# Linear attention and a gated unit on one core: the products of v and the folds of k of chunk 0 written out in one order for three engines

## The chip, the cores and the metric
The kernel runs on one core of one Trainium2 chip. The time is the device time of one execution, in microseconds. The core has a matrix engine (PE, TensorE) that writes to eight banks of PSUM, a vector engine (DVE), a scalar engine (ACT), a third elementwise engine (POOL, GpSimd) and SP (SyncE), which here issues all DMAs.

## What is computed
All inputs are float32; x is 2048 x 1024. `xn` is x normalized row by row. Two branches come from it:

```python
xn = layernorm(x)
q, k, v = split(xn @ wqkv)                     # 32 heads of 32
phi(a) = [softmax(a @ w_phi), softmax(-(a @ w_phi))]   # per head
o = phi(q) @ (phi(k).T @ v) / (phi(q) @ sum(phi(k)) + 1e-6)
s = o @ wo
g = silu((sigmoid(xn @ w_gate) * (xn @ w_up)) @ w_down)
out = x + s * g
```

## The kernel before
**Products.** A float32 value is split into a high part, a cast to PE's reduced float type (ACT, L126), and the rest, the value minus the high part (DVE, L127). `mm3` (L129 to L133) then makes three matmuls of 128 x 128 by 128 x 512 of one product: high by high, high by low, low by high. Every large matrix product is done block by block with seven products in place of eight (B11, T2, T3, B21, T1, T4, B22), whose operands are sums and differences of the blocks of both sides. B21 adds to the bank of B11, T4 to that of T3, B22 to that of T1, so each of these must wait until the first result has been read out.

**Stages.** The 2048 rows are two chunks of 1024. Chunk 0 goes through the projections v, k, q (in this order, `PROJ`), seven products each in the order B11, B21, T2, T3, T4, T1, B22 (`order`, L289), and then the gated unit; chunk 1 follows, with attention work laid in between; then `w_down`, the attention output and `wo`. One of the seven products of a projection has four banks (`u`, 128 rows each) of four `mm3` each: 48 matmuls. `proj_out` (L384 on) reads the banks: ACT copies B11 and B21 (L396, L399), DVE adds the others up (L393) and SP stores results to `qkv_d`.

**The opening.** The kernel starts on raw x. `norm` (L156 to L179) takes statistics of a tile of 128 rows on DVE (L163, L164), a square root on ACT (L169), a reciprocal on DVE (L170), six small operations on POOL (L172 to L177) and one normalization of 1024 columns on ACT (L179). `transpose` (L189 to L201) has PE turn a tile in eight 128 x 128 transposes (L195) and ACT copy them out (L199). `x_sums` (L203 to L209) makes the operands T1 to T4 of x: T2 and T3 on DVE, T1 and T4 on POOL. `v_sums` (L250 to L257) makes those of the weights of v, half on DVE and half on POOL, 1024 columns at a time. The weights of k and q are first multiplied by `w_phi`, once for all: `fold` (L274 to L285) loads four blocks of 128 x 512, has PE multiply each by block-diagonal `bd` in four matmuls (L283), copies the results (L284), and `w_sums` (L225 to L234) stores three blocks as they are, makes four sums in place on POOL (L229 to L232) and stores these, all to `wf_d`. The first sum overwrites the fourth block, which has been stored before. Four such `fold(K, k)` and four `fold(Q, k)` fill what is needed; the folds of q use slots (50, 51) and (52, 53) in turn.

**What sets the order.** The entries of `side`, in the order x tiles, `v_sums`, x tiles, four folds of k, the remaining operands of x (`x_rest`), four folds of q, are started one by one by `step()` after each bank of v's products, so all of them are done within v. A scheduler then puts the instructions of each engine in one order; `issue_after` bars an instruction from standing ahead of another. `prep` (L338 on) loads and splits weights for the products to come, as far as a ring of eight slots (28 to 35) has room. During k, after B11, T2, T4 and B22 (n = 7, 9, 11, 13), one task of `bg2` is started each time: `o_sums` (L261 to L271), which loads four raw blocks of `wo` into slots (52, 53) or (45, 46) by turns, splits three of them, makes four sums of them on POOL, splits these too, and stores each of the seven splits to `wo_d` from one of four slots (`o_split`: 54, 36, 37, 38). Before it starts, PE is warmed with 28 transposes of the identity (L729).

Of the kernel before, what the change touches and what calls it, by code (L numbers as in the profile page):

```python
# [48 lines left out]
def hedgehog_glu_kernel(  # L49
# [19 lines left out]
    make_identity(nc, ident)  # L69

# [35 lines left out]
    WARM = 28  # L106
# [17 lines left out]
    def split(o, src):  # L124

        nc.scalar.copy(o[0], src)  # L126
        return nc.vector.tensor_sub(o[1], src, o[0].bitcast(F32))  # L127
# [22 lines left out]
    last_norm, last_chain = [], []  # L150

    def x_load(t, slot):
        nc.sync.dma_start(whole(slot), x[t * P:(t + 1) * P, :])
        return whole(slot)

    def norm(tiles, xs):  # L156
        n = len(tiles)
        st = small.tile([P, 2, 2, 6], F32, name=f"bn{tiles[0]}", tag="bn")
        mv = small.tile([P, 2, 2], F32, name=f"mv{tiles[0]}", tag="mv")
        ws = small.tile([P, 4, 2], F32, name=f"lnw{tiles[0]}", tag="lnw")  # L160
        for i, xt in enumerate(xs):
            for a in range(2):
                nc.vector.bn_stats(st[:, i, a], xt[:, a * HB:(a + 1) * HB])  # L163
            nc.vector.bn_aggr(mv[:, :, i], st[:, i])  # L164
        v, r, a, b = [ws[:, q, :n] for q in range(4)]
# [4 lines left out]
        nc.vector.reciprocal(r, a)  # L170

        eng.tensor_mul(a, r, r)  # L172
# [4 lines left out]
        last_chain[:] = [eng.tensor_scalar(b, b, -1.0, None, op0=ALU.mult).ins]  # L177
        for i, xt in enumerate(xs):
            last_norm[:] = [nc.scalar.activation(xt, xt, AF.Identity, bias=b[:, i:i + 1], scale=r[:, i:i + 1]).ins]  # L179

    def operand(c, i, u, b):

        if c == 0:
            o, cs = run(XO[i], 4), slice(u * P, (u + 1) * P)
            split((o[:, :, 0, cs], o[:, :, 1, cs]), b.rearrange("p (k t) -> p k t", t=P))
        else:
            nc.sync.dma_start(xo_d[i, :, u], b)

    def transpose(t, xt, dst):  # L189

        c, th, u = t // CTT, t % CTT // 4, t % 4
        for q in range(2):
            tp = tps.next()
            for k in range(4):
                nc.tensor.transpose(tp[:, k * P:(k + 1) * P], xt[:, (4 * q + k) * P:(4 * q + k + 1) * P], ident)  # L195
            i = {(0, 0): B11, (1, 0): B21, (1, 1): B22}.get((q, th))
            if c == 0 and th == 0:
                operand(c, i, u, tp)
            nc.scalar.copy(dst[q], tp)  # L199
            if c and i is not None:  # L200
                operand(c, i, u, dst[q])  # L201

    def x_sums(c, u, first, second):  # L203
        (b11, b21), (b12, b22) = first, second
        t2 = b22 if c else b12
        for i, o, a, b in ((T1, b11, b12, b11), (T3, b12, b22, b12), (T2, t2, b22, b11), (T4, b21, b21, t2)):
            (nc.vector if c == 0 and i in (T2, T3) else nc.gpsimd).tensor_sub(o, a, b)
            if c or i in (T2, T3):
                operand(c, i, u, o)  # L209
# [12 lines left out]
    fraw = Ring(halves(43, 11))  # L222
    fblock = {K: Ring(((4, 5), (6, 7))), Q: Ring(((50, 51), (52, 53)))}
# [13 lines left out]
    VA = (39, 41, 45, 36)  # L237
    v_first = {B11: 39, B21: 41, T2: 39, T3: 45, T4: 39, T1: 36, B22: 41}
# [4 lines left out]
    def v_block(f, kh):  # L243
        return wv[kh * HB:(kh + 1) * HB, f * HB:(f + 1) * HB].rearrange("(k p) n -> p k n", p=P)
# [5 lines left out]
    def v_sums():  # L250
        vec, pool = nc.vector.tensor_tensor, nc.gpsimd.tensor_tensor
        for f, o, a, b, op in ((vec, 3, 2, 3, "add"), (vec, 2, 0, 2, "subtract"),
                               (pool, 0, 3, 0, "subtract"), (pool, 1, 1, 0, "subtract")):
            for h in range(2):
                f(whole(VA[o] + h), whole(VA[a] + h), whole(VA[b] + h), op=getattr(ALU, op))
        for i in (T2, T3, T1, B22):
            nc.sync.dma_start(wf_d[V, i], row4(v_first[i]))  # L257
# [15 lines left out]

    def fold(which, k):  # L274

        bs = halves(*fblock[which].next())
        for b, (f, h) in zip(bs, ((0, 0), (0, 1), (1, 0), (1, 1))):
            r = fraw.next()
            nc.sync.dma_start(r, wqkT[which, f, k + 4 * h].rearrange("p g n -> p (g n)"))
            ps = tps.next()  # L280
            for g in range(4):
                gs = slice(g * P, (g + 1) * P)
                nc.tensor.matmul(ps[:, gs], r[:, gs], bd[:, 4 * f + g], start=True, stop=True)  # L283
            nc.scalar.copy(b, ps)  # L284
        w_sums(lambda i, b: nc.sync.dma_start(wf_d[which, i, :, k], b), *bs)  # L285
# [52 lines left out]
    def prep():  # L338
# [9 lines left out]
        if kind == "proj":  # L348
            h = len(ready[n]) // 2
            if h == 0:  # L350
                here = c == 0 and what == V
                proj_src[n] = r = v_first[i] if here else proj_raw.next()
                if what == V and i in (B11, B21, T4) and not (here and i != T4):
                    nc.sync.dma_start(row4(r), v_block(*{B11: (0, 0), B21: (0, 1), T4: (1, 1)}[i]))
                elif not here:
# [153 lines left out]
    def x_task(t):  # L509
        xt = x_load(t, 52)  # L510
        norm([t], [xt])
        th, u = t % CTT // 4, t % 4
        transpose(t, xt, halves(53 + th))
        if th:
            x_sums(t // CTT, u, halves(53), halves(54))
# [178 lines left out]
    XS = (24, 25, 26, 27, 52, 53, 24, 25)  # L694
    first = [halves(i) for i in (50, 51, 54, 38)]
    b12s, b22s = Ring(halves(10)), halves(8, 9)
    xts = [x_load(0, XS[0])]
    phraw = whole(47)[:, :KT * DH].rearrange("p (g f) -> p g f", f=DH)
    nc.sync.dma_start(phraw, w_phi.rearrange("(g p) f -> p g f", p=P))
    v_load(0)  # L700
    xts += [x_load(t, XS[t]) for t in range(1, 4)]
    v_load(1)
    xts += [x_load(t, XS[t]) for t in range(4, 6)]

    def x_tiles(*tiles):
        norm(tiles, [xts[t] for t in tiles])
        for t in tiles:
            if t < 4:
                transpose(t, xts[t], first[t])
            else:  # L710
                b = b12s.next(), b22s[t - 4]
                transpose(t, xts[t], b)
                x_sums(0, t - 4, first[t - 4], b)
            if t < 2:
                xts.append(x_load(t + 6, XS[t + 6]))
            if t == 1:
                v_load(2)
                v_load(3)

    def x_rest():  # L720
        for i, name, src in ((B22, "x1", b22s), (T1, "x2", [b[0] for b in first]), (T4, "x6", [b[1] for b in first])):
            block(name, XO[i], 4, F32R)
            for u in range(4):
                operand(0, i, u, src[u])
        fraw.items = halves(43, 54)


    for n in range(WARM):
        nc.tensor.transpose(banks[3][:, n % 4 * P:(n % 4 + 1) * P], ident, ident)  # L729
    with tc.high_priority():  # L730
        x_tiles(0)
    with tc.issue_after(last_norm[0]):
        while prep():
            pass
# [5 lines left out]
    def phi_blocks():  # L740
        with tc.issue_after(last_chain[0]):
            for j in range(4):
                nc.gpsimd.tensor_copy(bd[j * DH:(j + 1) * DH, :, j * DH:(j + 1) * DH], phraw[j * DH:(j + 1) * DH])
# [9 lines left out]
    for k in range(4):  # L753
        todo(fold, K, k)
    todo(x_rest)
# [3 lines left out]
    pmm = Ring(banks[:4])  # L759
# [27 lines left out]
    for n, (kind, c, what, i) in enumerate(ops):  # L787
        ws = ready[n]
# [280 lines left out]
```

## Time and profile before
| | us |
|---|---|
| median of 3 runs (lowest, highest) | 2431.39 (2426.29, 2431.77) |
| the profiled execution | 2429.22 |
| its span in the trace | 2427.4 |
| PE busy in the span | 2378.9 |
| DVE, ACT, POOL busy | 1761.4, 1028.7, 991.4 |
| mean granted clock of PE | 0.994 of full speed |

In rows of the profile, a line number is that of the kernel before, `out<-in` are tiles by name with buffer numbers left out, `x16` is a count of instructions. In the order of time, the first two numbers are start and duration in us, and a bracket at the end gives how long the engine had been idle and who ended that. `x`, `fa`, `fb`, `fc`, `p`, `w` are blocks of slots in SBUF: fc holds slots 47 to 54, fb 43 to 46, p 36 to 38, fa 39 to 42, w 28 to 35, x 0 to 27. In a row of a DMA (SPq) the duration is that of the issue; a view of DMAs adds the time from issue to landing.

### The profile page before, as it was taken

What the parts mean: (1) busy time and instruction counts of PE and PEld (TensorE: products, weight loads), DVE (VectorE), ACT (ScalarE), POOL (GpSimd) and SP (SyncE); (2) the same over time, 40 slices, a digit from 0 to 9 for tenths busy, and PEclk for the clock granted to TensorE, in tenths of its full rate; (3) what the DMA queues carried; (4) which work ended last, traced back from release to release, by engine and by line L of the source; (5) the groups of instructions that cost most, each with busy time, mean ns of one, the idle gap of its engine ahead of it and who ended that gap; (6) DMA issues with size and microseconds to landing.
All of it is one profiled execution on the core that took longest, in us unless ns stands there. A gap on an engine that the chain in (4) does not pass through costs nothing.

```text
span 2427.4 us, 31881 instructions
## 1 busy us (share of the span) xinstructions
PE 2378.9 (98%) x10948; PEld 1972.9 (81%) x10948; DVE 1761.4 (73%) x2311; ACT 1028.7 (42%) x1535; POOL 991.4 (41%) x661
## 2 busy tenths in 40 slices
PE   7999999999999999999999999999999999999998
PEld 6887888888888878888888888888888888878776
DVE  6645577777777579747867888746888988866776
ACT  6443244445444344314444444433443334454443
POOL 5542245665666441222343222223333435314554
PEclk8999999999999999999999999999999999999999
DMA  7898767777776787777778666576667666877554
GB/s 271 274 344 317 248 235 255 267 262 255 261 264 251 248 286 254 253 268 250 258 249 284 216 222 217 199 268 241 221 222 243 218 220 217 286 250 251 181 185 134
DMA packets 232659, 597.34 MB, mean 246 GB/s; under 512 B 30512, under 2 KB 30512, under 8 KB 227888
## 3 DMA queue, kind: packets, MB, share of 16 engines
q1 hardware_dynamic: 232496, 595.30, 71.3%
q8 instruction: 86, 1.41, 0.2%
q14 instruction: 77, 0.63, 0.1%
HBM read 360.05 MB, written 235.14 MB: 245 GB/s over the span
## 4 chain that ended last, share of the span: by engine, by line
PE 83%; DMA 6%; DVE 5%; issue 2%; ACT 1%; POOL 1%; SPq 0%; DVEq 0%; ACTq 0%; POOLq 0%
PE bank L131 26%; PE bank L133 26%; PE bank L132 26%; DMA fc<-xo_d 1%; PE bank L463 1%; PE bank L283 1%; DVE w L127 1%; PE bank L635 1%; DVE x L127 1%; PE bank L653 1%; PE bank L195 1%; DVE p L127 1%; DMA fc<-e_d 0%; DMA fb<-wqkT 0%; DMA wo_d<-fc 0%
## 5 line engine op out<-in xcount | busy, mean ns | idle before, releaser
L131 PE MATMUL bank<-x,w 128*128 128x512 f32 x2352 | 912.1, 390 | 3.7 <-ACT x L126 1.6
L132 PE MATMUL bank<-x,w 128*128 128x512 f32 x2352 | 915.6, 389 | 0.0
L133 PE MATMUL bank<-x,w 128*128 128x512 f32 x2352 | 907.2, 389 | 0.0
L126 ACT CAST w<-fa 128x512 fp32r<-128x512 f32 (+1 forms) x444 | 308.4, 698 | 547.6 <-PE bank L132 377.5
L131 PEld LDWEIGHTS bank<-x,w 128*128 128x128 f32 x2352 | 441.5, 188 | 96.7 <-ACT x L126 2.0
L133 PEld LDWEIGHTS bank<-x,w 128*128 128x128 f32 x2352 | 441.6, 188 | 91.8 <-DVE w L127 0.4
L127 DVE TENSOR_TENSOR w<-fa,w 128x512 fp32r<-128x512 f32 (+1 forms) x444 | 435.5, 985 | 110.9 <-ACT w L126 105.0
L132 PEld LDWEIGHTS bank<-x,w 128*128 128x128 f32 x2352 | 441.7, 188 | 90.2
L131 PE MATMUL bank<-w,x 128*128 128x512 f32 x708 | 279.2, 395 | 7.5 <-DVE fb L393 2.6
L133 PE MATMUL bank<-w,x 128*128 128x512 f32 x708 | 279.1, 394 | 2.2 <-DVE x L127 2.2
L132 PE MATMUL bank<-w,x 128*128 128x512 f32 x708 | 278.6, 394 | 0.4 <-DVE w L127 0.4
L857 POOL TENSOR_TENSOR fb<-fb,fc 128x512 f32<-128x512 f32 x57 | 88.6, 1555 | 238.6 <-DVE fc L856 213.6
L131 PEld LDWEIGHTS bank<-w,x 128*128 128x128 f32 x708 | 134.4, 190 | 36.6 <-ACT x L126 4.6
L133 PEld LDWEIGHTS bank<-w,x 128*128 128x128 f32 x708 | 134.1, 189 | 30.5 <-DVE x L127 3.7
L592 POOL TENSOR_TENSOR fc<-fc 128x1024 f32<-128x1024 f32 x32 | 82.3, 2571 | 183.8 <-ACT fc L428 128.7
L132 PEld LDWEIGHTS bank<-w,x 128*128 128x128 f32 x708 | 134.2, 190 | 28.1 <-DVE w L127 0.9
L127 DVE TENSOR_TENSOR w<-fb,w 128x512 fp32r<-128x512 f32 (+1 forms) x114 | 106.2, 931 | 39.2 <-ACT w L126 37.7
L856 DVE TENSOR_TENSOR fc<-fc,bank 128x512 f32<-128x512 f32 x84 | 57.4, 684 | 101.2 <-PE bank L133 91.6
L127 DVE TENSOR_TENSOR x<-fa,x 128x512 fp32r<-128x512 f32 x112 | 114.0, 1018 | 20.4 <-ACT x L126 20.4
L126 ACT CAST w<-fb 128x512 fp32r<-128x512 f32 (+1 forms) x114 | 71.4, 626 | 133.5 <-PE bank L132 102.6
L604 POOL TENSOR_TENSOR fc<-fc,sa 128x1024 f32<-128x1024 f32 x32 | 70.0, 2189 | 98.3 <-DVE sa L601 98.3
L126 ACT CAST p<-fc 128x512 fp32r<-128x512 f32 (+1 forms) x86 | 64.1, 750 | 104.7 <-DVE fc L444 61.9
(258 smaller groups left out, 3224.5 us busy)
## 6 DMA issues: line engine op xcount, KB each, us to landing
ws_d<-w SPq DMA_DIRECT2D x112, 512.0 KB, 3.8
w<-ws_d SPq DMA_DIRECT2D x112, 512.0 KB, 5.1
fa<-w_gu SPq DMA_DIRECT2D x84, 512.0 KB, 4.1
fa<-h_d SPq DMA_DIRECT2D x84, 512.0 KB, 4.1
fa<-wf_d SPq DMA_DIRECT2D x32, 1024.0 KB, 6.6
h_d<-fc SPq DMA_DIRECT2D x120, 256.0 KB, 3.4
fc<-e_d SPq DMA_DIRECT2D x48, 512.0 KB, 3.8
fc<-qkv_d SPq DMA_DIRECT2D x80, 256.0 KB, 4.5
```

The lines of the kernel that those rows point to most:

```text
L126: nc.scalar.copy(o[0], src)
L127: return nc.vector.tensor_sub(o[1], src, o[0].bitcast(F32))
L131: nc.tensor.matmul(o, a[0], b[0], start=first, stop=False, **kw)
L132: nc.tensor.matmul(o, a[0], b[1], start=False, stop=False, **kw)
L133: nc.tensor.matmul(o, a[1], b[0], start=False, stop=last, **kw)
L195: nc.tensor.transpose(tp[:, k * P:(k + 1) * P], xt[:, (4 * q + k) * P:(4 * q + k + 1) * P], ident)
L283: nc.tensor.matmul(ps[:, gs], r[:, gs], bd[:, 4 * f + g], start=True, stop=True)
L463: nc.tensor.matmul(kvb[g // 2][:, g % 2 * 256:g % 2 * 256 + 256], v[:, g].rearrange("p a f -> p (a f)"), ph[:, g].rearrange("p a f -> p (a ...
L592: nc.gpsimd.tensor_mul(ez, e, zb)
L604: nc.gpsimd.tensor_mul(e3, e3, r2[:, :, None].to_broadcast([P, 32, DH]))
L856: v = nc.vector.tensor_add(b, u2 if q == 3 else u1, bank)
L857: nc.gpsimd.tensor_mul(g, g, b)
```

## The change
The opening of chunk 0 up to the end of v is no longer left to `side`, `prep` and the scheduler. A string `FIRST` lists some 290 steps by short names (`bn` statistics, `sq`/`rc`/`ch` the scale, `n` normalization, `T` transposes, `k` copies of them, `xh`/`xl` high and low parts of x, `wh`/`wl` those of the weights, `s` and `T.s` sums of weights and of x, `m` half of a bank's products, `e` evacuation, `F` and `c` a fold of k and its copy, `phi` the blocks of `bd`), and `in_order` chains the instructions that they make on PE, DVE and ACT, each after the one before on its engine. All later work is tied to stand behind the last of each (`after_first`).

- Scale: POOL's six operations become four fused ones on DVE; x tile 0 is loaded and normalized in two halves; statistics, scale and normalization are steps of their own.
- All sums of x and of the weights of v are on DVE (T2 of x now from T3 instead of from B12).
- The folds of k are part of the order, one block at a time, with slots of their own for raw and folded blocks. The folds of q are now the only entries of `side`, so they are started after the first banks of k.
- In the order of the built program, the last fold of q stands on PE after 455 products instead of after 323.
- 33 warming transposes instead of 28; the first weights come in two halves; `w_phi` is loaded after x and the weights of v.

```diff
-    WARM = 28
+    WARM = 33
-        eng = nc.gpsimd if tiles[0] < CTT else nc.vector
-        eng.tensor_scalar_add(v, mv[:, 1, :n], EPS_LN)
-        nc.scalar.activation(a, v, AF.Sqrt)
-        nc.vector.reciprocal(r, a)
-
-        eng.tensor_mul(a, r, r)
-        eng.tensor_mul(a, a, v)
-        eng.tensor_scalar(b, a, -0.5, 1.5, op0=ALU.mult, op1=ALU.add)
-        eng.tensor_mul(r, r, b)
-        eng.tensor_mul(b, mv[:, 0, :n], r)
-        last_chain[:] = [eng.tensor_scalar(b, b, -1.0, None, op0=ALU.mult).ins]
...
+        def rest():
+
+            fused(a, v, EPS_LN, r, op0=ALU.add, op1=ALU.mult)
+            fused(a, a, -0.5, r, op0=ALU.mult, op1=ALU.mult)
+            fused(r, a, 1.5, r, op0=ALU.add, op1=ALU.mult)
+            fused(b, mv[:, 0, :n], -1.0, r, op0=ALU.mult, op1=ALU.mult)
...
-    fraw = Ring(halves(43, 11))
-    fblock = {K: Ring(((4, 5), (6, 7))), Q: Ring(((50, 51), (52, 53)))}
+    fblock = {K: ((6, 7), (36, 37), (52, 53), (36, 37)), Q: ((50, 51), (52, 53)) * 2}
+
+    fraw = {K: halves(43) * 4 + [slots[i][:, 1] for i in (50, 51, 54, 38)] + halves(43) +
+            [slots[i][:, 1] for i in (54, 38)], Q: halves(43, 54) * 4}
...
-    v_first = {B11: 39, B21: 41, T2: 39, T3: 45, T4: 39, T1: 36, B22: 41}
+    v_first = {B11: 39, B21: 41, T2: 26, T3: 45, T4: 36, T1: 39, B22: 41}
...
+    def v_sum(i, h):
+
+        a, b, op = {T3: (39, 45, ALU.subtract), T2: (36, 45, ALU.subtract), T1: (26, 39, ALU.add),
+                    B22: (41, 26, ALU.subtract)}[i]
+        nc.vector.tensor_tensor(whole(v_first[i] + h), whole(a + h), whole(b + h), op=op)
...
     def fold(which, k):
 
-        bs = halves(*fblock[which].next())
-        for b, (f, h) in zip(bs, ((0, 0), (0, 1), (1, 0), (1, 1))):
-            r = fraw.next()
-            nc.sync.dma_start(r, wqkT[which, f, k + 4 * h].rearrange("p g n -> p (g n)"))
+        bs = halves(*fblock[which][k])
+        for n in range(4):
+            fold_load(which, k, n)
             ps = tps.next()
-            for g in range(4):
-                gs = slice(g * P, (g + 1) * P)
-                nc.tensor.matmul(ps[:, gs], r[:, gs], bd[:, 4 * f + g], start=True, stop=True)
-            nc.scalar.copy(b, ps)
-        w_sums(lambda i, b: nc.sync.dma_start(wf_d[which, i, :, k], b), *bs)
+            folded(which, k, n, ps)
+            nc.scalar.copy(bs[n], ps)
+        fold_sums(which, k)
...
+    FIRST = """
+        bn0a bn0b bn0 sq0 whB110 rc0 ch0 wlB110 n0q0 n0q1 T00 T01 bn1 k01 xh00 bn2 sq1 xh01 k00 whB111 rc1 ch1 xl00
+        n1 wlB111 mB1100 whB210 bn3 T10 mB1101 xh10 whB211 xl10 T11 xl01 sq2 mB1110 eB110 rc2 ch2 k10 wlB210 n2
...
+        mT111 wlB220 mT120 eT11 wlB221 mB2210 mB2211 mT121 F30 eT12 mB2220 c30 c22 mB2221 F31 eB222 eB221 F32 F33
+        mT100 c33 c31 c32 mT101 mT130 eT10 mT131 mB2200 eT13 mB2201 mB2230 mB2231 eB223 eB220""".split()
...
+    def do_sum(i, u):
+        u = int(u)
+        o, a, b = {"3": (t3s[u], b22s[u], b12s[u]), "2": (t2s[u], t3s[u], first[u][0]),
+                   "4": (first[u][1], first[u][1], t2s[u]), "1": (first[u][0], b12s[u], first[u][0])}[i]
+        (nc.vector.tensor_add if i == "2" else nc.vector.tensor_sub)(o, a, b)
...
+    with in_order(mybir.EngineType.PE, mybir.EngineType.DVE, mybir.EngineType.Activation):
+        for name in FIRST:
+            f, found = next((f, m) for form, f in forms for m in [re.fullmatch(form, name)] if m)
+            f(*found.groups())
+    flow.update(item=14, made=28, used=28)
...
+    with after_first():
+        while prep():
+            pass
 
     def todo(f, *a):
-        side.append(lambda: f(*a))
-
-    todo(x_tiles, 1)
-    todo(lambda: (x_tiles(2, 3), phi_blocks()))
-    todo(x_tiles, 4, 5)
-    todo(v_sums)
-    todo(x_tiles, 6, 7)
-    for k in range(4):
-        todo(fold, K, k)
-    todo(x_rest)
+        def entry():
+            with after_first():
+                f(*a)
+        side.append(entry)
+
     for k in range(4):
         todo(fold, Q, k)
...
     for n, (kind, c, what, i) in enumerate(ops):
+        if n < len(order):
+            continue
```

More of the change, by code (lines that the diff above doesn't have):

```diff
@@ L148, in hedgehog_glu_kernel @@
     tps = Ring(banks[4:])
-    last_norm, last_chain = [], []
     def x_load(t, slot):
@@ L181, in operand @@
[L181 to L193, printed above, removed]
-            for k in range(4):
[L195 to L201, printed above, removed]
@@ new lines, in operand, with by_k, transposed, x_sums @@
+    def operand(i, u):
+        o, cs = run(XO[i], 4), slice(u * P, (u + 1) * P)
+        return o[:, :, 0, cs], o[:, :, 1, cs]
+    def by_k(b):
+        return b.rearrange("p (k t) -> p k t", t=P)
+    def transposed(t, q, xt, tp):
+        for k in range(4):
+            nc.tensor.transpose(tp[:, k * P:(k + 1) * P], xt[:, (4 * q + k) * P:(4 * q + k + 1) * P], ident)
+    def x_sums(u, first, second):
+        (b11, b21), (b12, b22) = first, second
+        for i, o, a, b in ((T1, b11, b12, b11), (T3, b12, b22, b12), (T2, b22, b22, b11), (T4, b21, b21, b22)):
+            nc.gpsimd.tensor_sub(o, a, b)
+            nc.sync.dma_start(xo_d[i, :, u], o)
@@ L510, in x_task @@
         xt = x_load(t, 52)
-        norm([t], [xt])
+        norm(t, xt)
         th, u = t % CTT // 4, t % 4
-        transpose(t, xt, halves(53 + th))
+        for q in range(2):
+            tp, b = tps.next(), slots[53 + th][:, q]
+            transposed(t, q, xt, tp)
+            nc.scalar.copy(b, tp)
+            i = {(0, 0): B11, (1, 0): B21, (1, 1): B22}.get((q, th))
+            if i is not None:
+                nc.sync.dma_start(xo_d[i, :, u], b)
         if th:
-            x_sums(t // CTT, u, halves(53), halves(54))
+            x_sums(u, halves(53), halves(54))
     dsteps = [(i, j, (0, 1)) for i in order[:-1] for j in range(NJ)]
@@ L690, in attend @@
         return out
-    XS = (24, 25, 26, 27, 52, 53, 24, 25)
+    XS = (4, 5, 6, 7, 52, 53, 24, 25)
     first = [halves(i) for i in (50, 51, 54, 38)]
-    b12s, b22s = Ring(halves(10)), halves(8, 9)
-    xts = [x_load(0, XS[0])]
-    phraw = whole(47)[:, :KT * DH].rearrange("p (g f) -> p g f", f=DH)
-    nc.sync.dma_start(phraw, w_phi.rearrange("(g p) f -> p g f", p=P))
[L700 to L734, printed above, removed]
+    b22s, b12s, t2s, t3s = halves(8, 9), halves(10, 11), halves(4, 5), halves(52, 53)
+    xts = [whole(i) for i in XS]
+    for a in range(2):
+        nc.sync.dma_start(slots[XS[0]][:, a], x[:P, a * HB:(a + 1) * HB])
+    for h in range(2):
+        nc.sync.dma_start(slots[39 + h], v_block(0, 0)[:, 2 * h:2 * h + 2])
+    for t in range(1, 4):
+        x_load(t, XS[t])
+    v_load(1)
+    for t in range(4, 8):
+        x_load(t, XS[t])
+    v_load(2)
+    v_load(3)
+    phraw = slots[27][:, 1, :KT * DH].rearrange("p (g f) -> p g f", f=DH)
+    nc.sync.dma_start(phraw, w_phi.rearrange("(g p) f -> p g f", p=P))
+    for n in range(2):
+        fold_load(K, 0, n)
     one = whole(44)[:, :P]
```

203 lines of the change are left out of this document (166 added, 37 removed).

## The prediction
> **What bounds the kernel now.** I read the page's busy shares first, then TensorE's (PE's) busy time by stretches, then PE's order of time where it is not full, then the engines it waited for. Of a stretch's row the first number is its length, the second PE busy with its count of records; the third number from the end is the granted clock.
> ```profile
> PE 2378.9 (98%) x10948; PEld 1972.9 (81%) x10948; DVE 1761.4 (73%) x2311; ACT 1028.7 (42%) x1535; POOL 991.4 (41%) x661
> ...
> 0.00:9.41 9.41, 5.79 (x29) 5.56 (x29) 1.66 (x4) 4.31 (x5) 3.23 (x15) 1.00 0.79 253
> 9.41:190.05 180.64, 166.09 (x848) 139.65 (x848) 103.08 (x124) 88.25 (x139) 93.07 (x84) 0.94 0.85 298
> 190.05:200.00 9.95, 7.41 (x33) 6.17 (x34) 8.33 (x11) 3.52 (x5) 0.45 (x1) 1.00 0.77 277
> 200.00:2427.40 2227.40, 2199.62 (x10041) 1821.50 (x10039) 1648.33 (x2173) 932.61 (x1387) 894.61 (x562) 1.00 0.70 242
> ```
> After 200 us PE is busy 2199.6 of 2227.4 us, so whatever the change takes from or adds to PE's time before that moves the end by the same amount. The same work is done in both kernels up to the end of product T3 of k, which stands at 190.05 here: 528 products (7 of v and 4 of k, 48 each), 64 transposes, 128 fold matmuls that show as two records each: together the 848 of the row. Their prices at full clock, by what starts next:
> ```profile
> 31.33 1.91 PE L195 MATMUL bank<-ident,x 128*128 128x128 f32 x16
> 32.99 0.48 PE L131 MATMUL bank<-w,x 128*128 128x512 f32 x1
> ...
> 94.17 1.05 PE L283 MATMUL bank<-fb,fb 128*128 128x128 f32 x8
> 94.97 0.48 PE L132 MATMUL bank<-w,x 128*128 128x512 f32 x1
> ...
> 179.67 0.39 PE L131 MATMUL bank<-w,x 128*128 128x512 f32 x1
> ...
> 189.65 0.39 PE L133 MATMUL bank<-w,x 128*128 128x512 f32 x1
> ```
> A transpose is (32.99 - 31.33) / 16 = 0.104 us, a fold record (94.97 - 94.17) / 8 = 0.10, a product (189.65 - 179.67) / 44 = 0.227 (45 rows stand from the first to the last). So 528 x 0.227 + 64 x 0.104 + 256 x 0.10 = 152 us of work in 180.6: 28.6 us are lost between the first transpose and the end of T3, and nothing beyond this can be won there. Where they go:
> ```profile
> 9.41 1.38 PE L195 MATMUL bank<-ident,x 128*128 128x128 f32 x8 [2.15 <-ACT x L179]
> ...
> 16.55 0.80 PE L133 MATMUL bank<-w,x 128*128 128x512 f32 x1 [2.20 <-DVE x L127]
> ...
> 18.42 0.63 PE L131 MATMUL bank<-w,x 128*128 128x512 f32 x1
> 18.84 0.63 PE L132 MATMUL bank<-w,x 128*128 128x512 f32 x1
> ...
> 23.33 1.64 PE L195 MATMUL bank<-ident,x 128*128 128x128 f32 x8 [2.49 <-ACT x L179]
> ...
> 52.25 3.68 PE L195 MATMUL bank<-ident,x 128*128 128x128 f32 x16 [3.62 <-ACT x L199]
> 55.72 1.92 PE L283 MATMUL bank<-fb,fb 128*128 128x128 f32 x8
> ...
> 81.39 1.13 PE L283 MATMUL bank<-fb,x 128*128 128x128 f32 x8 [1.79 <-DMA x<-wqkT]
> ```
> Waits for normalized and transposed rows of x (2.49, 3.62), for split operands (2.20), for raw weights of the folds (1.79), and a halved clock after the gaps: products 0.42 apart at 18.42, the 16 transposes of 52.25 taking 3.47 us to the next start instead of 1.66.
>
> **What the change does there.** (1) The scale of a tile goes from six small POOL operations to four fused VectorE (DVE) ones, and tile 0 comes and is normalized in halves. On POOL the six take 6.47 to 8.08:
> ```profile
> 6.47 0.20 POOL L172 TENSOR_TENSOR lnw<-lnw 128x1 f32<-128x1 f32 x1 [0.52 <-DVE lnw L170]
> ...
> 7.85 0.23 POOL L177 TENSOR_SCALAR lnw<-lnw 128x1 f32<-128x1 f32 x1
> 8.11 1.24 ACT L179 ACTIVATE x<-x,lnw 128x1024 f32<-128x1024 f32 x1 [1.92 <-POOL lnw L177]
> ```
> Four DVE steps at some 0.2 us are 0.8 instead of 1.6, and half a normalization is 0.6 instead of 1.24: the first transpose comes 1.5 us sooner. (2) The 2.49 wait (tile 1, same POOL chain) and the 3.62 wait (tiles 6 and 7 late) are planned away: 6.1. (3) With the second gap goes its half clock: 3.47 - 1.66 = 1.8 on the transposes and about 1.4 on the two fold groups up to 58.83. Sum: 1.5 + 6.1 + 3.2 = 10.8, so **-11**. I leave the rest in: the first product still needs the same splits, and weights of the folds still come late, now for single fold groups between products. The eight x sums (T1, T4) and four v-sum passes that move from POOL to DVE add about 8 x 0.69 + 4 x 1.21 = 10 us to DVE, from 0.69 rows beside no POOL operation; DVE is busy 103 of 181 us, so they hide, unless the order makes them late. Bounds of this term: 0 (DVE takes the place of POOL) to -20 (two thirds of the loss).
> ```profile
> 57.42 0.69 DVE L127 TENSOR_TENSOR x<-x,x 128x512 fp32r<-128x512 f32 x1
> 58.14 1.65 DVE L207 TENSOR_TENSOR x<-x,fc 128x512 f32<-128x512 f32 x1
> ```
>
> **What it moves.** The folds of q leave v. Before, the last one stands on PE after 323 of the 336 products of v; in the built order of the changed kernel it stands after 455 products, in T2 of k. From there to the first product of T4 of k are 205 products before and 73 after. This matters, since T4 adds to the banks of T3, so it waits for T3's evacuation by DVE (L393, after: L408), and ahead of that on DVE stand splits of the two first `o_sums` tasks, whose raw blocks of `wo` go into slots 52 and 53: the ones in which the last fold of q still lies. The chain in the rows of before:
> ```profile
> 142.50 1.05 PE L283 MATMUL bank<-fb,fc 128*128 128x128 f32 x8
> 143.59 0.59 ACT L284 COPY fc<-bank 128x512 f32<-128x512 f32 x1 [5.13 <-PE bank L283]
> 151.87 5.81 SPq L264 DMA_DIRECT2D fc<-wo  x4
> 158.65 0.62 ACT L126 CAST p<-fc 128x512 fp32r<-128x512 f32 x1 [1.48 <-DMA fc<-wo]
> 172.92 0.68 DVE L127 TENSOR_TENSOR p<-fc,p 128x512 fp32r<-128x512 f32 x1
> 178.69 0.62 ACT L126 CAST p<-fb 128x512 fp32r<-128x512 f32 x1 [5.94 <-DMA fb<-wo]
> 184.38 0.68 DVE L127 TENSOR_TENSOR p<-fb,p 128x512 fp32r<-128x512 f32 x1
> 185.14 1.29 POOL L229 TENSOR_TENSOR fb<-fb 128x512 f32<-128x512 f32 x1 [17.88 <-DVE p L127]
> 190.04 1.01 DVE L127 TENSOR_TENSOR fc<-fb,fc 128x512 fp32r<-128x512 f32 x1 [4.99 <-ACT fc L126]
> 190.97 0.68 DVE L127 TENSOR_TENSOR p<-fb,p 128x512 fp32r<-128x512 f32 x1
> 191.75 0.69 DVE L393 TENSOR_TENSOR fb<-fc,bank 128x512 f32<-128x512 f32 x1
> 192.59 0.47 PE L131 MATMUL bank<-w,x 128*128 128x512 f32 x1 [2.56 <-DVE fb L393]
> ```
> Read down: last fold ends at 143.55; its copy, its POOL sums and stores free the slots; wo is loaded; task 0's seven splits end at 173.6; task 1's first three splits, POOL sums and next two splits; then the evacuation; then T4 at 192.59, 49.0 us after the fold. The 205 products beside it are 46.5 us, so only 2.56 us show. After, 73 x 0.227 = 16.6 us lie beside it. All of task 0's seven and five of task 1's splits stand between T2's and T3's evacuations on DVE in the new order (before: task 1's five). Task 1's blocks are loaded ahead of task 0's, so that wait (173.6 to 178.69) goes: 30.1 us to task 0's end, about 2.5 for three splits, 192.59 - 185.14 = 7.5 for the rest: 40 us. The last fold is now the block that the first POOL sum overwrites, so its store must land first; I add 2.5 of the 4.9 that such a store takes:
> ```profile
> wf_d<-fc SPq DMA_DIRECT2D x28, 256.0 KB, 4.9
> ...
> DMA to landing us min/median/max: 2.6/5.5/6.1
> ```
> Stall: 42.5 - 16.6 = **26 us** (the last row: loads of wo). Bounds: 13, if each step is as short as its row lets it (three groups of four POOL sums at 1.29, store and load at 2.6, splits at 0.7: some 30 us), to 37 (all 49 and 4.9). The old 2.56 goes. After so long a gap the clock is halved for a while; 3.8 us from 23.33 to 27.1 cost about 2 us, so **+2** (0 to 3.4). The Trainium skill (TensorE: Matmul & The Clock Gate, Part 1) says that an idle window of about 3.4 us halves the clock until a busy one: the rows at 23.33 and 52.25 agree; its figure would give 1.7 us, an estimate.
>
> The chain works only if DVE cannot take T3's evacuation ahead of the splits. In the rows it did not: T3's first bank was full 36 products before 190.05, at 181.9, DVE sat idle for 4.99 us until 190.04, and the evacuation came behind the split of 190.97 all the same. The same page (Architectural detail) calls the queues of ScalarE and VectorE strict FIFO; these rows agree.
>
> **Sum**, against the profiled execution's own 2429.2 us (span 2427.4): -11 + 26 - 2.6 + 2 = +14.4. That execution lies 2.2 below the median of the three runs, 2431.4, so I set 2431.4 + 14 = **2445**. Later parts: the same operations; PE has no other gap to give.
>
> **Rivals.** (a) Faster: the chain from the last fold is shorter than the 19 us that would reproduce the old stall, so only the opening counts: 2431 - 11 = 2420. It decides at 16.6 + 13 = 30 us of chain, where gain and stall cancel. Against it: 30 us is the sum of shortest rows. (b) No change: chain near that point, stall about 11 to 17: 2424 to 2438. (c) DVE becomes the bound of the opening: its order is fixed by hand, it takes over the sums, and beside a POOL operation a 512-wide sum takes 1.65 instead of 0.69 (rows above), with 16 POOL sums of the k folds now inside v. Then -11 becomes 0: 2456. For it: DVE at 8.5 to 8.9 of 10 us from 10 to 30 already; against: 57% over the stretch. The Trainium skill (SBUF — State Buffer, Who interferes with whom) says that a sum with both inputs in SBUF and a POOL operation lock each other out whole; here the DVE one takes 0.96 longer, less than the POOL sum's 1.29. (d) The plan does not do what it says: k's first product waits, as the folds of k end later in v; a 1 MB load of wf_d and two split passes would give up to 9 us: 2454.
>
> **Chances.** Forecast (+7 to +24): 0.60. (c) and (d): 0.14. (b): 0.17. (a): 0.09. A difference within 0.3%, 7.3 us, can't be told from none. Faster 0.08, same 0.18, slower 0.74. The range leaves out (a) and the far ends of the stall: 2432 to 2457.
>
> **What would show it.** Right: PE starts its first transpose near 8; no gap above 2 us between 18 and 70; T3 of k ends near 179; then one gap of 20 to 30 us before the first product of T4, ended by DVE's evacuation, with twelve splits of `o_sums` ahead of it on DVE; clock 0.5 in the slice behind it. Wrong: that gap under 13 us; DVE without idle time from 20 to 100 and PE waiting for its lows; a gap at k's first product.

## The result and the profile after

The changed kernel takes 2451.7 us (median of six runs, 2445.1 to 2455.3) where the kernel before takes 2429.0 in the same comparison: a ratio of 1.0091, 95% interval 1.0072 to 1.0109, so it is 22.7 us slower. The forecast was 2445 (2432 to 2457). The profiled execution took 2454.9 with a span of 2453.2.

PE's busy time by stretches, cut at the first transpose, at the end of T3 of k and at the first product of T4 (columns as in the prediction):
```profile
9.74:182.49 172.75, 165.13 (x848) 139.52 (x848) 99.11 (x146) 81.69 (x128) 47.01 (x31) 0.94 0.76 268
182.49:211.69 29.20, 0.00 (x1) 0.03 (x1) 15.93 (x16) 9.07 (x14) 13.86 (x10) 0.54 0.83 297
211.69:2453.20 2241.51, 2208.80 (x10072) 1829.10 (x10072) 1637.58 (x2155) 935.14 (x1388) 890.08 (x563) 1.00 0.70 240
```
The same 848 records now stand in 172.75 us instead of 180.64, and behind them PE does nothing for 29.2 us. The waits of PE (what it waited for, us in total, times, longest) up to 240 us name what ends that gap, and what else is left:
```profile
PE bank L134 <- DVE fb L408: 29.2, 1, 29.2
PE bank L288 <- DMA fb<-wqkT: 5.3, 3, 2.7
PE bank L203 <- ACT x L794: 1.6, 1, 1.6
...
PE bank L136 <- DVE x L816: 1.1, 1, 1.1
```
The long one is T4 of k, and it waits for T3's evacuation, as before (2.56 there). In order of time, up to T4 (start, duration, engine, line, tiles, and how long the engine had been idle):
```profile
164.15 2.21 SPq L268 DMA_DIRECT2D fb<-wo  x4
166.93 4.91 SPq L291 DMA_DIRECT2D wf_d<-fc  x7
167.46 1.29 POOL L233 TENSOR_TENSOR fc<-fc 128x512 f32<-128x512 f32 x1
...
179.38 1.29 POOL L232 TENSOR_TENSOR fc<-fc 128x512 f32<-128x512 f32 x1 [7.89 <-DMA wf_d<-fc]
186.04 2.97 SPq L268 DMA_DIRECT2D fc<-wo  x3
187.74 0.62 ACT L129 CAST p<-fc 128x512 fp32r<-128x512 f32 x1 [4.19 <-DMA fc<-wo]
188.45 0.69 DVE L130 TENSOR_TENSOR p<-fc,p 128x512 fp32r<-128x512 f32 x1 [1.77 <-ACT p L129]
189.45 1.26 POOL L232 TENSOR_TENSOR fc<-fc 128x512 f32<-128x512 f32 x1 [3.85 <-DMA fc<-wo]
200.31 0.69 DVE L130 TENSOR_TENSOR p<-fc,p 128x512 fp32r<-128x512 f32 x1 [0.57 <-ACT p L129]
201.57 0.69 DVE L130 TENSOR_TENSOR p<-fb,p 128x512 fp32r<-128x512 f32 x1 [0.57 <-ACT p L129]
209.41 1.53 DVE L130 TENSOR_TENSOR p<-fb,p 128x512 fp32r<-128x512 f32 x1
210.87 1.27 DVE L408 TENSOR_TENSOR fb<-fc,bank 128x512 f32<-128x512 f32 x2
211.69 0.77 PE L134 MATMUL bank<-w,x 128*128 128x512 f32 x1 [29.22 <-DVE fb L408]
```
Read down: the last fold's sums start at 179.38, although its matmuls ended near 165.9; they wait for a store of the same block, which SP issued at 169.27 as one of the seven of 166.93 to 171.84. Then come the load of `wo` into slots 52 and 53 (tile `fc`), task 0's seven splits to 201.0, five of task 1's in slots 45 and 46 (tile `fb`), and T3's evacuation, which writes into 45 and 46 too.

Where the time lies, by the start of the n-th product (512 columns) in the two traces:

| product | what starts | before | after | difference |
|---|---|---|---|---|
| 96 | T2 of v | 58.8 | 48.8 | -10.1 |
| 144 | T3 of v | 79.2 | 60.7 | -18.5 |
| 336 | k | 146.4 | 124.0 | -22.4 |
| 480 | T3 of k | 179.0 | 171.4 | -7.6 |
| 528 | T4 of k | 192.6 | 211.7 | +19.1 |
| 576 | T1 of k | 203.6 | 224.4 | +20.8 |
| 3000 | chunk 0's unit | 759.5 | 782.9 | +23.4 |
| 9600 | near the end | 2377.4 | 2404.4 | +27.0 |

The 22 us at 336 contain the folds of q, which left v. At 480 both have done the same work: the opening is worth 7.6. The stall gives 29.2 less the old 2.56, the half clock behind it 1.7. The few us after that are treated below.

### The profile page after: what moved, and what is told of

Same layout as the page of the kernel before. It is cut to its first block, busy times and chain, and to the rows that moved or that the text cites. A ratio compares the mean times of both kernels' runs of the same rounds, so it can differ in the third digit from the quotient of the medians.

```text
span 2453.2 us, 31840 instructions
## 1 busy us (share of the span) xinstructions
PE 2380.5 (97%) x10953; PEld 1975.0 (81%) x10953; DVE 1755.8 (72%) x2323; ACT 1030.9 (42%) x1536; POOL 952.8 (39%) x611
## 4 chain that ended last, share of the span: by engine, by line
PE 82%; DVE 7%; DMA 6%; issue 2%; ACT 1%; POOL 1%; SPq 0%; ACTq 0%; DVEq 0%; POOLq 0%
PE bank L134 26%; PE bank L135 26%; PE bank L136 26%; DVE w L130 1%; PE bank L478 1%; PE bank L288 1%; DMA fc<-xo_d 1%; PE bank L656 1%; PE bank L674 1%; DVE p L130 1%; DVE x L130 1%; DMA fc<-qkv_d 1%; DMA fb<-w_down 1%; DMA wf_d<-fc 1%; DMA fc<-e_d 1%
## 5 line engine op out<-in xcount | busy, mean ns | idle before, releaser
L129 ACT CAST w<-fa 128x512 fp32r<-128x512 f32 (+1 forms) x434 | 298.2, 690 | 582.4 <-PE bank L135 377.7
L130 DVE TENSOR_TENSOR w<-fa,w 128x512 fp32r<-128x512 f32 (+1 forms) x434 | 422.8, 979 | 125.9 <-ACT w L129 120.0
L134 PE MATMUL bank<-w,x 128*128 128x512 f32 x708 | 280.6, 397 | 33.0 <-DVE fb L408 29.2
L129 ACT CAST w<-fb 128x512 fp32r<-128x512 f32 x112 | 69.3, 619 | 136.6 <-PE bank L135 106.2
L130 DVE TENSOR_TENSOR w<-fb,w 128x512 fp32r<-128x512 f32 x112 | 98.3, 878 | 32.2 <-ACT w L129 27.4
```

The costliest lines, as they stand in the source:

```text
L134: nc.tensor.matmul(o, a[0], b[0], start=first, stop=False, **kw)
```

## The experiments

**Theory.** The late folds of q hold slots 52/53; the first `o_sums` task waits for them; the second, in 45/46, waits behind the first; and since T3's evacuation writes into 45/46, it stands behind that task's splits. Rivals: the traffic of the moved folds; the fixed order with its sums on DVE; DVE's queue, whatever the slots.

**e1_one_pair.** All `o_sums` tasks in 52/53, so that 45/46 are free for T3.
```diff
-    bg2.extend([lambda k=k: o_sums(k, halves(*((52, 53), (45, 46))[k % 2])) for k in range(4)])
+    bg2.extend([lambda k=k: o_sums(k, halves(52, 53)) for k in range(4)])
```


> The changed kernel with the raw blocks of all four o_sums tasks in slots 52 and 53; slots 45 and 46, into which product T3 of k writes its evacuated sums, are used by no o_sums task. Folds of q, loads, splits and stores stay as many and start from the same places. Theory (late q folds hold slots 52/53, the o_sums tasks behind them hold slots 45/46, and these hold T3's evacuation): in the built order T3's four evacuations now stand ahead of every split of o_sums, so the first product of T4 of k waits for nothing (under 2 us instead of 29.2), the half clock behind it goes, and the time is that of the changed kernel less 29.2 and 1.7: 2421 us (2417 to 2426), ratio to the kernel before 0.997. Rival 1 (VectorE's queue as such: splits that wait for the late loads stand ahead of some evacuation whatever slot they use): four splits now stand ahead of T4's last evacuations, so the wait comes back at the first products of T1, shorter by the 48 products of T4 (11 us): 10 to 18 us there, 2432 to 2440. Rival 2 (the traffic of the moved folds, or the plan of v, makes T4 late): the wait at T4 stays, 2445 to 2452.

Measured: 2421.4 us, ratio to the kernel before 0.9977 (0.9968 to 0.9985). DVE around T3's evacuation, in order of time:
```profile
178.75 0.69 DVE L408 TENSOR_TENSOR fb<-fc,bank 128x512 f32<-128x512 f32 x1 [2.04 <-PE bank L136]
...
182.34 0.68 DVE L408 TENSOR_TENSOR fb<-fc,bank 128x512 f32<-128x512 f32 x1
184.46 0.69 DVE L130 TENSOR_TENSOR p<-fc,p 128x512 fp32r<-128x512 f32 x1 [1.44 <-ACT p L129]
```
The four evacuations now come as the banks fill, the first split of `o_sums` after them, and PE's wait for DVE's evacuations up to 260 us is 0.2 us in all, at T1 too. There are as many loads, splits and folds as in the changed kernel, so neither their traffic nor the fixed order nor DVE's queue makes the stall by itself. The median falls by 30.3 us (27.7 by the two ratios to the kernel before, since that kernel's own median is 2.3 lower in this comparison); the theory said 30.9.

**e2_q_folds_late.** The kernel before, with one part of the change alone: the folds of q start with k.
```diff
-    for k in range(4):
-        todo(fold, Q, k)
...
+        if n == 7:
+            for k in range(4):
+                todo(fold, Q, k)
```


> The kernel before, and only the four folds of q are held back until the products of k begin; v is as before, without the plan, and the o_sums tasks use the pairs 52/53 and 45/46 as before. In the built order the last fold of q stands 99 products ahead of the first product of T4 of k (205 in the kernel before, 73 in the changed one). Theory: the chain from that fold to T3's evacuation was 46 us in the changed kernel (165.6 to 211.7), 99 products are 22.5 us, so T4 waits some 20 us (15 to 27) instead of 2.56, with a half clock of about 2 behind it: 2429 + 20 = 2449 us (2441 to 2458), ratio 1.008. Rival (the fixed order of the three engines and its sums on VectorE cause the wait): no wait above 4 us at T4, 2425 to 2433.

Measured: 2456.9, ratio 1.0130 (1.0116 to 1.0144). T4's first product, and ACT in front of it:
```profile
219.81 0.76 PE L131 MATMUL bank<-w,x 128*128 128x512 f32 x1 [29.67 <-DVE fb L393]
```
```profile
190.34 0.62 ACT L126 CAST p<-fc 128x512 fp32r<-128x512 f32 x1 [9.99 <-DMA fc<-wo]
...
211.56 0.62 ACT L126 CAST fc<-fb 128x512 fp32r<-128x512 f32 x1 [6.77 <-DMA wo_d<-fc]
```
The late folds make the stall by themselves, without the plan: the cause is right. Its size is not: 29.7 where 20 was worked out (15 to 27), since the chain is not of a fixed length: it is 52.1 us here (167.7 to 219.8), against 45.8 in the changed kernel. Here ACT waits 6.8 us within it for a store of a split.

**e3_swap_pairs.** Tasks 0 and 2 in 45/46, 1 and 3 in 52/53.
```diff
-    bg2.extend([lambda k=k: o_sums(k, halves(*((52, 53), (45, 46))[k % 2])) for k in range(4)])
+    bg2.extend([lambda k=k: o_sums(k, halves(*((45, 46), (52, 53))[k % 2])) for k in range(4)])
```
This changes part of the computation: task 2's blocks overwrite T3's sums before T1 has added to them.

> The changed kernel with the two pairs of raw blocks swapped: tasks 0 and 2 of o_sums in slots 45/46, tasks 1 and 3 in 52/53. The pair that waits for the last fold of q now belongs to task 1, and no task that waits for it stands ahead of T3's evacuation; in the built order ten splits of it stand between the evacuations of T4 and those of T1. Theory: no wait above 6 us at T4; the wait moves to the first product of B22, which adds to the banks of T1, and is there what the chain leaves beyond T4 and T1 (96 products, 21.8 us): 5 to 25 us, time 2428 to 2448. Rival (queue order alone, first task first): the wait at T4 stays above 15 us. Rival (traffic or plan): it stays at 29 us and 2452.

Measured: 2445.3, ratio 1.0082 (1.0066 to 1.0097). PE's longest wait:
```profile
228.55 0.77 PE L134 MATMUL bank<-w,x 128*128 128x512 f32 x1 [24.81 <-DVE fb L408]
```
At T4 PE no longer waits; 96 products later, at B22, it waits 24.8 us. On DVE the seven splits of task 1, which now has the late slots (198.04 to 213.9), and five of task 2 in 45 and 46 (218.51 to 227.8) stand in front of T1's evacuation, which adds to 45 and 46. The wait follows the slots. It is at the upper end of what was expected.

**e4_tasks_in_q.** The `o_sums` tasks start within q.
```diff
-            if (i in (B21, T2, T1)) if c else n in (7, 9, 11, 13):
+            if (i in (B21, T2, T1)) if c else n in (14, 16, 18, 20):
```

> The changed kernel with the four o_sums tasks started after products of q (14, 16, 18, 20 of the list) instead of k (7, 9, 11, 13); slots as in the changed kernel. Theory: nothing of o_sums stands in k, so the wait at T4 of k goes as a whole (under 2 us). The tasks in 45/46 then stand beside T3 of q and ahead of the gates of the first up product, which use 45 to 47: a wait of up to 5 us at T4 of q and of 5 to 15 at the first up products. Time 2425 to 2445. Rival (traffic of the folds, or the plan): the wait at T4 of k stays above 15 us and 2445 to 2455.

Measured: 2441.0, ratio 1.0060 (1.0046 to 1.0074). Waits of PE up to 420 us:
```profile
PE bank L134 <- ACT fb L1008: 11.7, 1, 11.7
...
PE bank L134 <- DVE fb L408: 3.3, 1, 3.3
```
Nothing is left at T4 of k; 3.3 us come at T4 of q and 11.7 in front of a gate of the unit behind it (L1008, `fb` again: slots 45 to 47). Against the kernel before it stands at -10.5 us at T1 of k, -5.3 at the end of q and +10.4 at product 1200. Other users of the pair pay.

**e10_q_blocks_swapped.** The last fold of q in 50/51, the one ahead of it in 52/53.
```diff
-    fblock = {K: ((6, 7), (36, 37), (52, 53), (36, 37)), Q: ((50, 51), (52, 53)) * 2}
+    fblock = {K: ((6, 7), (36, 37), (52, 53), (36, 37)), Q: ((52, 53), (50, 51)) * 2}
```

> The changed kernel, with the two pairs of blocks of the folds of q swapped: the last fold lies in slots 50 and 51, and the one ahead of it in 52 and 53, where the raw blocks of wo go. Theory A (the slots alone carry the chain, as the prediction had it): the sums of the last-but-one fold started 13.3 us earlier on POOL than those of the last (166.09 and 179.38 in the changed kernel), so the loads of wo come that much earlier and the wait at T4 of k falls from 29.2 to 16 to 20 us. Theory B (POOL, which takes the last fold's sums ahead of those of o_sums in any case, carries it): POOL is free for task 0 at 185.6 instead of 189.45, so the wait falls by 1 to 4 us only, to 25 to 28.

Measured: one run, 2453.2; the wait at T4 is 25.3 us. POOL:
```profile
177.19 1.29 POOL L232 TENSOR_TENSOR fc<-fc 128x512 f32<-128x512 f32 x1 [5.72 <-DMA wf_d<-fc]
...
184.01 2.24 POOL L232 TENSOR_TENSOR fc<-fc 128x512 f32<-128x512 f32 x1 [1.10 <-DVE w L130]
```
The first load of `wo` into 52 was issued 7.9 us sooner (175.96, after: 183.84), but POOL takes the last fold's sums (177.19) first in any case and task 0's only at 184.01, 5.4 sooner than in the changed kernel; the wait falls by 3.9 (theory B). So the slots tie task 0 to the folds, but in this order POOL's queue ties it nearly as well.

**The opening.** The other question was why it brought 7.6 instead of 11. In the changed kernel PE waits at 75.68 and 80.45 for raw weights of the second fold of k; here is what SP does in front of that, then POOL:
```profile
63.14 7.03 SPq L291 DMA_DIRECT2D wf_d<-x  x4
70.26 0.38 SPq L261 DMA_DIRECT2D wf_d<-fa  x1
70.73 0.41 SPq L282 DMA_DIRECT2D fb<-wqkT  x1
```
```profile
59.18 3.94 POOL L232 TENSOR_TENSOR x<-x 128x512 f32<-128x512 f32 x1 [55.84 <-DMA wf_d<-x]
63.19 2.16 POOL L233 TENSOR_TENSOR x<-x 128x512 f32<-128x512 f32 x1
...
67.65 2.17 POOL L235 TENSOR_TENSOR x<-x 128x512 f32<-128x512 f32 x1
```
```profile
66.10 1.05 PE L288 MATMUL bank<-fb,fb 128*128 128x128 f32 x8
...
75.68 2.08 PE L288 MATMUL bank<-fb,fb 128*128 128x128 f32 x8 [2.17 <-DMA fb<-wqkT]
80.45 2.08 PE L288 MATMUL bank<-fb,fb 128*128 128x128 f32 x8 [2.70 <-DMA fb<-wqkT]
```
The raw block was free at 67.2 (66.10 + 1.05), the load into it was issued at 70.73: SP stood for 7 us behind four stores of the first fold, each waiting for a POOL sum. And POOL's four sums took 10.6 us, 2.14 to 3.94 each, where most of the others take 1.29.

**e5_two_loads_out**, on top of e1: no loads for the last two blocks of the second fold.
```diff
-        f, r = FB[n][0], fraw[which][4 * k + n]
+        f, r = FB[n][0], fraw[which][4 * k + (n % 2 if (which, k) == (K, 1) else n)]
...
-                 (0, 3): (1, 1), (1, 0): (1, 2), (1, 1): (1, 3),
+                 (0, 3): (1, 1),
```


> On top of e1_one_pair. Leaves out the loads of the last two raw blocks of the second fold of k; their matmuls read the two blocks that are already there, so the matmuls, copies, sums and stores stay as many. Theory (the opening brought 7.6 instead of 11 because these two loads come late: they are issued by SP behind stores that wait for POOL's sums, and land beside two stores of 1 MB): the two waits for raw weights between 72 and 80 us (2.1 and 3.3 in e1) go, and with them the half clock behind them (6.8 us long, some 2 us): e1 less 5 to 7, 2415 us (2413 to 2418). Rival (the waits hide another lateness, of VectorE's or ScalarE's planned order): a wait of about the same size comes at a following product of T4 or T1 of v, 2419 to 2423.

Measured: 2417.6, ratio 0.9958 (0.9945 to 0.9972). Both waits and the half clock are gone, and T4 of v starts 7.6 us before e1's, of which 1.0 was there at the start of T3; at T1 of v 2.8 come back (a wait for an evacuation). So the two late loads cost some 6.6 us at T4 of v, of which 4.5 are left at T3 of k; both theory and rival hold a part.

**e6_norm_first**, on top of e1: in the order, `whB110` behind `n0q0`.
```diff
-        bn0a bn0b bn0 sq0 whB110 rc0 ch0 wlB110 n0q0 n0q1 T00
+        bn0a bn0b bn0 sq0 rc0 ch0 n0q0 whB110 wlB110 n0q1 T00
```


> On top of e1_one_pair, one step of the planned order moved: the first split of the weights of v on ScalarE stands behind the normalization of the first half of tile 0, not ahead of it. In the changed kernel the scale of tile 0 was ready at 6.92 us, but ScalarE took up the normalization at 8.87, behind a split that waited for weights until 7.92. Theory (the forecast first transpose near 8 failed by this order alone): the first transposes of tile 0 come at 8.1 to 8.6, where the 33 opening transposes end. The first product needs the splits of weights too, which come 0.5 to 1 us later now, so of the 1.5 us little reaches the end: e1 less 0 to 1.5, 2420.5 us (2419 to 2422). Rival (the first transpose sets the opening): all of 1.5 to 2 us reach T3 of k, 2419.5.

Measured: 2421.8, ratio 0.9976 (0.9965 to 0.9987). In the changed kernel ACT and PE ran
```profile
7.92 1.04 ACT L827 CAST w<-fa 128x1024 fp32r<-128x1024 f32 x1 [1.97 <-DMA fa<-wv]
8.87 1.52 ACT L794 ACTIVATE x<-x,lnw 128x512 f32<-128x512 f32 x2
```
```profile
9.74 1.69 PE L203 MATMUL bank<-ident,x 128*128 128x128 f32 x8 [1.65 <-ACT x L794]
```
and now
```profile
6.92 0.81 ACT L794 ACTIVATE x<-x,lnw 128x512 f32<-128x512 f32 x1 [1.01 <-DVE lnw L174]
```
```profile
7.78 0.66 PE L203 MATMUL bank<-ident,x 128*128 128x128 f32 x4 [1.08 <-ACT x L794]
```
The first transpose is 2 us sooner, the first product 1.4 sooner than e1's, and at the end of T3 of k 0.1 is left: other waits of the opening set that time.

**e7_loads_ahead**, on top of e1: POOL's sums and the stores of the first fold of k behind the second fold's last two loads (a step `f0` behind `F11`, and an order on SP).
```diff
-        if all((k, m) in copied for m in range(4)):
+        if k and all((k, m) in copied for m in range(4)):
...
+    def do_f0():
+        w_sums(lambda i, b: behind(nc.sync.dma_start(wf_d[K, i, :, 0], b)), *halves(*fblock[K][0]))
...
```


> On top of e1_one_pair: the four POOL sums and seven stores of the first fold of k stand behind the second fold's last two loads on SP, instead of ahead of them; all loads and stores stay. Theory (SP takes its instructions in order, and the two loads wait there behind stores that wait for POOL): the loads are issued as soon as their blocks are free, near 66.6 and 69.6 us, and the two waits of 5.4 us together fall below 2. Whether the end sees it is open: the sums of the first fold start some 10 us later on POOL, and if what follows them in the planned order (copies of the folds on ScalarE, then the splits of T1) comes late, a wait of 3 to 8 us at T1 of v takes the gain back. 2415 to 2419 without that, 2420 to 2426 with it. Rival (the loads are late by traffic, not by order): the waits stay above 4 us.

Measured: 2421.9, ratio 0.9976 (0.9967 to 0.9986). PE's waits from 60 to 110 us, then ACT between them:
```profile
74.24 1.16 PE L295 MATMUL bank<-fb,fb 128*128 128x128 f32 x8 [0.90 <-DMA fb<-wqkT]
...
96.13 0.77 PE L134 MATMUL bank<-w,x 128*128 128x512 f32 x1 [6.25 <-DVE fc L415]
```
```profile
85.10 1.14 ACT L822 CAST x<-x 128x512 fp32r<-128x512 f32 x2 [9.08 <-DMA wf_d<-x]
```
Of the two waits 0.9 is left, so SP's order made the loads late. 6.25 come back at T1 of v, as the sums are late: ACT waits 9.08 us for the stores of the first fold (`wf_d<-x`) before it splits more of x, and DVE's evacuation in front of T1 comes behind these splits.

**e8_before_one_pair.** The kernel before, with e1's line only.

> The kernel before, and only the raw blocks of all four o_sums tasks in slots 52 and 53, as in e1_one_pair. Theory: T3's evacuation no longer stands behind splits of o_sums, so the wait of 2.56 us at the first product of T4 of k goes, and nothing else changes: the kernel before less 2.6, ratio 0.999. e1 less this one is then what the plan of v and the late folds of q bring by themselves, some 3 to 8 us. Rival (task 1 now waits for task 0's blocks, and comes late in a later place): 0 to 5 us slower than before.

Measured: 2422.8, ratio 0.9985 (0.9973 to 0.9997). The 2.56 at T4 are gone (0.4 in all is left for evacuations). By median e1 is 1.4 us faster than this (3 to 8 were expected), which the two intervals don't tell apart; by the trace it leads by 6.9 at the end of T3 of k and by 2.3 at product 9600. So no gain of the plan of v with its late folds is shown at the end as it stands.

**e9_early_loads**, on top of e1: the loads of the second fold moved ahead of SP's waiting stores, with POOL's sums left where they were.
```diff
-    fraw = {K: halves(43) * 4 + ...
+    fraw = {K: halves(43, 43, 24, 43) + ...
...
-        ... wlT40 F10 s1a mT310 eT30 xh6f mT311 xh4f T4s1 xl4f F11 wlT41
+        ... wlT40 F10 F11 s1a mT310 eT30 xh6f mT311 xh4f T4s1 xl4f wlT41
...
-        later = {(0, 0): (0, 2), (0, 1): (0, 3), (0, 2): (1, 0), (0, 3): (1, 1), (1, 0): (1, 2), (1, 1): (1, 3),
+        later = {(0, 0): (0, 2), (0, 1): (0, 3), (0, 2): (1, 2), (0, 3): (1, 3),
...
+        if (k, n) == (0, 1):
+            for m in range(2):
+                fold_load(K, 1, m)
...
```


> On top of e1_one_pair, nothing left out: the first two raw blocks of the second fold of k are loaded into slot 24, which is free after tile 6's transposes, and the last two into slot 43 behind the first fold's matmuls, so that these two loads stand ahead of the five stores that wait for POOL's sums; the second fold's second matmul group moves up behind its first. POOL's sums stay where they were (in e7 they came later, and a wait of 6.2 us at T1 of v took the gain back). Theory (the two loads are late by SP's order, and cost 5.4 us and a half clock): no wait above 1.5 us for raw weights between 60 and 85 us, no half clock there; a wait of 2 to 4 us at T1 of v as in e5, where the loads were left out; time as e5, 2417 us (2414 to 2419), ratio 0.996. Rival (e5 was faster since it moved less data): the waits come back in other places, 2420 to 2423.

Measured: 2414.6, ratio 0.9943 (0.9928 to 0.9958): faster than both kernels (the one before took 2427.9 in this comparison). PE's fold groups of that stretch and what waits behind them:
```profile
65.08 1.95 PE L289 MATMUL bank<-fb,x 128*128 128x128 f32 x16
72.32 1.95 PE L289 MATMUL bank<-fb,fb 128*128 128x128 f32 x16
...
91.10 0.77 PE L134 MATMUL bank<-w,x 128*128 128x512 f32 x1 [2.37 <-DVE fc L409]
```
No group waits for its raw weights, 2.4 come back at T1 of v, and T3 of k ends 11.8 us before the kernel before's (8.6 in e1, 7.6 in the changed kernel): about the 11 that the prediction had put down for the opening. Here nothing is left out, so what e5 gained was lateness, not bytes.

## Why the prediction came out

- **Opening, -11: the step that was too large; 7.6.** The two gaps of 2.49 and 3.62 are gone, with their half clocks, as foreseen: no wait over 2 us from 18 to 70 us. The 1.5 us at the first transpose did not come (9.74 instead of "near 8"): the scale was ready at 6.92, but ACT's written order had it split weights first, and e6 shows that this part is worth nothing later anyway. The failed step is "I leave the rest in": the folds' weights were costed at no change, and the two late loads with their half clock cost 6.6 at T4 of v (e5) and 3.2 at T3 of k (e9 against e1). I had counted POOL's fold sums as DVE's burden (rival c), not SP's: stores that wait for those sums stood ahead of the loads. That e9 comes to the forecast 11 is in part luck, since its sum is another one: the 1.5 is missing there too (first transpose at 9.49), and 2.4 are lost at T1 of v.
- **Stall, +26: right in place and sign; 29.2, with luck in the size.** The chain from the last fold to T4 was 45.8 us (165.9 to 211.7), not 42.5. The mis-sized term is the store ahead of the fold's first sum, put at 2.5, with 0.7 for the copy: from the last fold's end to that sum at 179.38 are 13.5 us. The copy ended at 167.0; SP issued the store at 169.27, behind stores of the fold before it; and the store took 10.0 us to land:
```profile
wf_d<-fc SPq DMA_DIRECT2D x1, 256.0 KB, 10.0
```
  In e1 the same store, issued at 168.64, took 4.9, which is what the prediction had for a whole one:
```profile
wf_d<-fc SPq DMA_DIRECT2D x1, 256.0 KB, 4.9
```
  In the changed kernel the four loads of `wo` into 45 and 46, which were free early, stood ahead of it on SP (164.15); in e1 no such load did. That they made it slow was not tried by itself. From 179.38 to task 0's end at 201.0 it took 21.6 where the prediction has 29.4 (30.1 - 0.7), 6 of the difference between the first sum and the first cast of `wo` (8.4, before: 14.4). So an error of +10.3 and one of -7.8 nearly cancel. The prediction also named slots 52 and 53 for both tasks. Task 1's lie in 45 and 46, with T3's sums, and e1 and e3 show that this is why DVE's order has the splits ahead of T3's evacuation.
- **Old wait, -2.6, and half clock, +2: right** (1.7: from +19.1 at T4's start to +20.8). The clock was 0.5 until 215.42, 3.7 us after PE had resumed (the number before the last two in a row):
```profile
184.70:215.42 30.72, 3.73 (x9) 3.00 (x10) 16.75 (x19) 8.65 (x14) 12.11 (x9) 0.50 0.85 308
215.42:225.66 10.24, 10.24 (x47) 8.46 (x46) 2.23 (x3) 2.10 (x2) 0.00 (x0) 1.00 0.15 59
```
  The Trainium skill (TensorE: Matmul & The Clock Gate, Part 1) has a busy window of about 3.4 us bring the clock back; the trace agrees.
- **"PE has no other gap to give": not quite.** The difference grows from 20.8 to 23.4 by product 3000, in three steps near 455, 572 and 689 us, with a fourth at 806. At each PE waits 0.6 us for a gate on ACT (L1008), which stands behind a table load (an instruction of 1.28 us on ACT):
```profile
PE bank L134 <- ACT fb L1008: 2.5, 4, 0.6
```
  The kernel before has such a table load there too (at 433.08) and PE does not wait, so the load alone isn't the cause. The same steps are in e1, not in e2 or e8, so they belong to the plan or the new scale, not to the late folds; which of these wasn't tried. What comes after that, up to 27.0, are small gaps and short half clocks that lie in other places in each trace; the medians differ by 22.7.
- **Rivals.** (c) did not happen: PE waits 1.1 us in all for low parts of x. (d) did not: k's first product waits for nothing. (a) and (b) needed a shorter chain.
- **The sum.** -7.6 + 29.2 - 2.6 + 1.7 = +20.7, where +14.4 was forecast. The opening and the stall missed the same way, so nothing cancelled between them; the range was wide enough for both.

## What to carry to other kernels

When a piece of work is moved, follow the buffers that it holds to the next user, and that user's buffers to the next, and add up what still lies between the end of the chain and the work that it can stop: here four small folds, the last of them moved by 132 products, turned a wait of 2.6 us into 29. A pair of blocks shared by a background task and an accumulator puts the accumulator behind the whole background chain; in the changed kernel one line that gave them different slots was worth more (some 28 to 30 us) than the rewritten opening (7.6), while in the kernel before, where the stall was small, it is worth 0.15% (e8). And a load should not stand on SP behind stores that wait for sums: in e9 moving two such loads ahead took the ratio from 0.9977 to 0.9943.

## What the runs showed of the hardware

- POOL's sums with DVE's two-input sums beside them (59 to 70 us) took 2.14 to 3.94 us instead of 1.29, and sums of 1024 columns on DVE up to 2.29 instead of 1.21:
```profile
58.40 1.21 DVE L258 TENSOR_TENSOR fa<-x,fa 128x1024 f32<-128x1024 f32 x1
...
66.36 2.29 DVE L258 TENSOR_TENSOR fa<-x,fa 128x1024 f32<-128x1024 f32 x1
```
  The Trainium skill (SBUF — State Buffer, Who interferes with whom) says that such operations lock each other out; in these rows POOL lost most. That this is why the stores came late is read from the rows; it was not tried by itself.
- Two gaps of 2.2 and 2.7 us, five us apart, went with a clock of 0.5 for 10.24 us in which PE was busy for 7.34, though neither gap is as long as the idle window of about 3.4 us that the Trainium skill (TensorE: Matmul & The Clock Gate, Part 1) names; in e7 one gap of 0.9 there left the clock full (the rows below, changed kernel and e7). The gap of 2.49 at 23.33 in the kernel before, which the prediction read as agreeing with that window, is shorter than it too:
```profile
75.48:85.72 10.24, 7.34 (x24) 6.30 (x25) 3.87 (x8) 4.23 (x8) 0.00 (x0) 0.50 0.79 275
```
```profile
70.00:90.00 20.00, 18.97 (x107) 16.29 (x105) 7.87 (x12) 7.25 (x12) 10.73 (x8) 1.00 0.82 293
```
